# Talking-heads attention and a gated feed-forward in one kernel: one more of a group's blocks split for fp32r, and bulk transfers moved within a step

## The chip, the cores and the metric

One core of one Trainium2 chip. The metric is the device time of one execution in microseconds (us). The core has a TensorE (PE, with its weight loads as PEld), a VectorE (DVE), a ScalarE (ACT), a GpSimd (POOL) and a SyncE (SP). Nearly all transfers of this kernel are issued by SP, one after the other, on one queue.

## The reference

What must be computed, cut to what matters: attention in which the scores of the 12 heads are mixed before the softmax and the probabilities are mixed after it, and a feed-forward with a piecewise quadratic gate on the result.

```python
# q, k, v: (4, 12, 448, 64); w_pre, w_post: (12, 12); w_in: (768, 2048); w_out: (2048, 768)
scores = q @ k^T / 8
scores = einsum('bhij,hg->bgij', scores, w_pre)      # first mixing
attn = softmax(scores, axis=-1)                      # minus the max, exp, over (sum + 1e-9)
attn = einsum('bhij,hg->bgij', attn, w_post)         # second mixing
x = (attn @ v), heads side by side                   # (1792, 768)
h = x @ w_in
g = where(h >= 1, h, where(h <= -1, 0, (h + 1)**2 / 4))
out = g @ w_out
```

## The kernel before

**Tiles, blocks, groups, steps.** The queries are cut into 16 tiles (`tiles`): three of 120 and one of 88 for each of the four batches. A tile's scores for all heads (`scores`, L169) are computed with the queries on the partitions and copied to a buffer `ssb`, half of the copies by DVE (L187) and half by ACT (L189). For the first mixing the rows must lie otherwise: ten queries times twelve heads on 120 partitions. `load_s` (L198) does that by a transfer from `ssb` to a tile `s10` (named s in the profile), one for each block of ten queries, 210 KB. A tile has 12 blocks (9 for the short ones), and each third of a tile is a group of 4 (or 3) blocks. There are 48 groups, and the loop at L893 works on one group in each step n.

**The first mixing** (`pre`, L214) multiplies a block by a 120x120 matrix that holds w_pre. It comes in two forms. A block as loaded is multiplied in fp32 (L223; two TensorE instructions in the trace). A block that DVE has split into a high and a low part of type fp32r (`split`, L205: a cast at L210 and a subtraction at L211) takes three fp32r matmuls (L221). Before the change, the blocks 1 and 3 of each group of 4, and block 1 of each group of 3, are split; the first group has no split blocks.

**One step n**, in the order in which its parts are issued (each engine takes its own in this order):

1. SP: `load_s` for the blocks of group n+1, in the order 1, 3, 0, 2.
2. PE: `pre` of the blocks of group n, in the order 0, 1, 2, 3, and transposes of keys and queries (`at`).
3. SP: loads of raw keys and queries for later (`mid`), then `conv_load(n+1)`, 768 KB of int64 weights.
4. DVE: the row maxima of group n (L226), then the split of the first of group n+1's blocks.
5. PE: `visit`, the product with v (`pv`, L306 and L311), which needs the double PSUM bank that DVE's copy of the last scores (L187) has freed; then the last 64 keys of the second mixing (L276).
6. ACT: exp (L232) and the scaling of the weights; POOL and DVE: 1/sum (L239) and the second mixing's matrices scaled by it (L243).
7. ACT and DVE: `turned` and `copies` (transposed keys and queries, split too; L166 is DVE's half for the queries), then DVE: the other splits of group n+1.
8. PE and ACT: `post`, the second mixing of group n-1 (L260, L262); then `conv_rest(n)` on ACT, DVE and POOL (L373 to L377).
9. SP: `conv_store(n-1)` (L381), 384 KB that POOL's L377 finished.
10. PE, DVE, ACT: `scores` of a third of the next tile (`vis`), with DVE's copy L187.
11. SP: `late`: `load_q` and `load_v` for later tiles, and `store_x` of a finished tile.

`conv_load` and its kin turn the int64 weights into fp32 ones in a DRAM buffer; they run in most of the steps, but not where the keys of the next batch are loaded. The loop's last steps (from n = 44, where `early` is false) also load the feed-forward's operands. After it comes the feed-forward (L547 and L712), in fp32r matmuls throughout.

**The start.** Before the loop, keys and queries of tile 0 are loaded, its scores computed, and v of batch 0 loaded (three calls of `load_v(0, g)`, L130 and L133: 384 KB and two of 32 KB each). Then comes `load_s` for group 0. v of batch 0 is first read by `pv` in step 4. `load_v` writes the tile in which the first keys lay.

The buffers: `s10` has 8, the split halves `sh` and `sl` 2 each, the PSUM ring `ps_l` has 6 banks, and the double bank of `pair` is one.

```python
for m in (*groups[n + 1][1::2], *groups[n + 1][::2]):
    load_s(m)
...
for m in ms:
    pre(m)
nxt = list(groups[n + 1][1::2]) if n + 1 < NG else []
...
if nxt:
    split(nxt.pop(0))
...
for m in nxt:
    split(m)
```

Of the kernel before, what the change touches and what calls it, by code (L numbers as in the profile page):

```python
# [9 lines left out]
F32 = mybir.dt.float32  # L10
F32R = mybir.dt.float32r
# [11 lines left out]
def tile_talking_heads_moe(  # L23
# [12 lines left out]
    B, H, S, D = q.shape  # L36
# [5 lines left out]
    KM = IB * H  # L42
# [16 lines left out]
    ap_ = s_att.enter_context(tc.tile_pool(name="att", bufs=2))  # L59
# [15 lines left out]
    for b in range(B):  # L75
        for i0 in range(0, S, QT):
            n = min(QT, S - i0)
            tiles.append((b, i0, n, -(-n // IB)))
    blocks = []
    groups = []  # L80
# [6 lines left out]
    NG = len(groups)  # L87
# [30 lines left out]
    def load_q(t, gs=(0, 1)):  # L118
        b, i0, n, nb = tiles[t]
        if 0 in gs:  # L120
            qraw[t] = qp.tile([128, H, D], F32, tag="qraw", name="qraw", bufs=2)
        for g in gs:
            h = slice(g * HP, (g + 1) * HP)
            nc.sync.dma_start(out=qraw[t][:n, h], in_=q[b, h, i0:i0 + n].rearrange("h p d -> p h d"))

    def load_v(b, g):
        t = ap_.tile([128, 4 * KC * D + 2 * D], F32, tag=f"v{g}", name=f"v{g}", bufs=1)
        x = t[:, :4 * KC * D].rearrange("p (h c) -> p h c", h=4)
        y = t[:, 4 * KC * D:].rearrange("p (s d) -> p s d", d=D)
        nc.sync.dma_start(out=x, in_=v[b, 4 * g:4 * g + 4, :SM].rearrange("h (p r) d -> p h (r d)", r=KC))  # L130
        for m in range(2):
            h = 4 * g + 2 * m
            nc.sync.dma_start(out=y[half[m]], in_=v[b, h:h + 2, SM:].rearrange("s p d -> p s d"))  # L133
        vt[b, g] = x, y
# [56 lines left out]
    s10 = {}  # L191
# [6 lines left out]
    def load_s(m):  # L198
        t, o, ni, c = blocks[m]
        n, nb = tiles[t][2:]  # L200
        x = ap_.tile([KM, S], F32, tag="s10", name="s10", bufs=8)
        nc.sync.dma_start(out=x[:ni * H], in_=ssb[t][o:n:nb])
        s10[m] = x

    def split(m):  # L205
        k = blocks[m][2] * H
        x = s10.pop(m)
        hi = ap_.tile([KM, S], F32R, tag="sh", name="sh", bufs=2)
        lo = ap_.tile([KM, S], F32R, tag="sl", name="sl", bufs=2)
        nc.vector.tensor_copy(out=hi[:k], in_=x[:k])  # L210
        nc.vector.tensor_tensor(out=lo[:k], in0=x[:k], in1=hi[:k].bitcast(F32), op=ALU.subtract)  # L211
        s10[m] = (hi, lo)
# [52 lines left out]
    def post_rest(ms):  # L265

        t, o, ni, c0 = blocks[ms[0]]
        a = place(t)[1]
        ps = ps_l.tile([128, HG, 2, 4 * IB], F32, tag="l", name="ps_r")
        n = 0  # L270
        for m in ms:
            t, o, ni, c = blocks[m]
            w = wr[m].rearrange("p (g m s) i -> p m g s i", m=2, s=2)
            n = c - c0 + ni
            for x, p in enumerate(half):
                nc.tensor.matmul(out=ps[p, :, :, c - c0:n], lhsT=ex[m][:, SM:], rhs=w[:, x, :, :, :ni],  # L276
                                 start=True, stop=True)

        def out():
            nc.scalar.activation(out=a[:, :, c0:c0 + n], in_=ps.rearrange("p g s c -> p (g s) c")[:, :, :n],  # L280
                                 func=AF.Copy)
        return out
# [13 lines left out]
    def pv(t, g, step):  # L296
        b, i0, n, nb = tiles[t]
        if g == 0:
            xo[t] = ap_.tile([128, HP, QT], F32, tag="xo", name="xo", bufs=2)
        ps = banks_x(step)  # L300
        to = [ps[0][:, m, :] for m in range(2)] if len(ps) == 1 else ps
        a, ar = aT[t]
        x, xr = vt[b, g]
        for s in range(2):
            for m, p in enumerate(half):
                nc.tensor.matmul(out=to[m][half[s], :n], lhsT=xr[p, s, :], rhs=ar[p, 2 * g + s, :n],  # L306
                                 start=True, stop=False)
        for m in range(2):
            for r in range(KC):
                for s in ((0, 1), (1, 0))[r % 2]:  # L310
                    nc.tensor.matmul(out=to[m][half[s], :n], lhsT=x[:, 2 * m + s, r * D:(r + 1) * D],  # L311
                                     rhs=a[:, r, 4 * g + 2 * m + s, :n], start=False, stop=(r == KC - 1))

        full = n - (IB - 1) * nb

        def out():
            for i, p in enumerate(ps):
                to = xo[t][:, 2 * g:2 * g + 2, :nb * IB]
                if len(ps) == 2:
                    to = to[:, i:i + 1]  # L320
                    p = p.unsqueeze(1)
                to = to.rearrange("p m (a o) -> p m a o", o=nb)
                nc.scalar.activation(out=to[:, :, :, :full],
                                     in_=p[:, :, :full * IB].rearrange("p m (o a) -> p m a o", a=IB),
                                     func=AF.Copy)
                if full < nb:
                    x = to[:, :, :IB - 1, full:]
                    y = p[:, :, full * IB:n].rearrange("p m (o a) -> p m a o", a=IB - 1)
                    nc.scalar.activation(out=x, in_=y, func=AF.Copy)
        return out  # L330

    def visit(n, rests):
        v = [lambda x=x: pv(*x, n) for x in vis2.pop(n, ())]
        if rests:
            v.insert(len(v) if n < NE else 0, lambda: post_rest(rests))
        return [f() for f in v]
# [46 lines left out]
    def conv(n, f):  # L383
        if n in CS and CS.index(n) < 2 * NF:
            f(CS.index(n))
# [372 lines left out]
    with tc.manual_schedule():  # L758
# [38 lines left out]
        for g in range(3):  # L797
            scores(0, [2 * g, 2 * g + 1], g == 1)
            if g < 2:
                for hp in range(2 * g + 2, 2 * g + 4):  # L800
                    trans_k(0, hp)()()
        for g in range(3):
            load_v(0, g)
        for g in range(2):
            trans_q(1, g)()()
        for m in groups[0]:
# [18 lines left out]
        mid = {}  # L825
        late = {}

        def put(n, f):
            late.setdefault(n, []).append(f)

        vis = {}
        vis2 = {}
        for g in range(2):
            put(0, lambda g=g: load_q(2, (g,)))
        for t in range(1, len(tiles)):
# [57 lines left out]
        for n in range(NG + 2):  # L893
            if n == NE:
                s_qk.close()
                s_se.close()
                pool['w'] = ctx.enter_context(tc.tile_pool(name="ffw", bufs=2, side="right",
                                                           reuse_waits="tile"))
                pool['ps_h'] = ctx.enter_context(tc.tile_pool(
                    name="ps_h", bufs=1, space=PSUM, side="right", reuse_waits="tile"))  # L900
            if n == NG - 1:
                s_ss.close()
            ms = groups[n] if n < NG else ()
            old = list(groups[n - 1]) if 0 < n <= NG else []
            if n + 1 < NG:
                for m in (*groups[n + 1][1::2], *groups[n + 1][::2]):
                    load_s(m)
            for f in loads.get(n, ()):
                f()
            if ms:  # L910
                sm = ap_.tile([KM, 4], F32, tag="sm", name="sm", bufs=3)
                nm = ap_.tile([KM, 4], F32, tag="nm", name="nm", bufs=3)
            for m in ms:
                pre(m)
            nxt = list(groups[n + 1][1::2]) if n + 1 < NG else []
            turned = [f() for f in [f() for f in at.pop(n, ())]]
            for f in mid.pop(n, ()):
                f()
            conv(n + 1, conv_load)
            for m in ms:  # L920
                row_max(m, nm[:, m - ms[0]:m - ms[0] + 1])
            if n == NG - 1:
                w0_lo()
            if nxt:
                split(nxt.pop(0))
            rests = list(old)
            early = n < NE
            copies = visit(n, rests) if early else ()
            for j, m in enumerate(ms):
                if j == 3 and old and not early:  # L930
                    post(old.pop(0))
                exps(m, j, sm)
            conv(n, conv_scaled)
            if ms:
                norm(ms, sm)
            for f in (*turned, *copies):
                f()
            for m in nxt:
                split(m)
            if n == NG:  # L940
                step(0)
            for m in old:
                post(m)
            conv(n, conv_rest)
            conv(n - 1, conv_store)
            if not early:
                for f in visit(n, rests):
                    f()
            for t, hps in vis.pop(n, ()):
                scores(t, hps)  # L950
            for f in late.pop(n, ()):
                f()
# [10 lines left out]
        for j in range(NJ):  # L963
# [70 lines left out]
            f = j - NJ + 3  # L1034
# [73 lines left out]
```

## Time and profile before

| | us |
|---|---|
| median of 3 runs | 874.63 |
| the three runs | 870.09, 874.63, 876.0 |
| the profiled execution, its own time | 873.21 |
| its span, first to last instruction | 871.5 |
| PE busy | 854.1 (98% of the span) |
| DVE busy | 645.1 (74%) |
| ACT busy | 565.2 (65%) |
| POOL busy | 212.4 (24%) |
| mean granted TensorE clock | 0.998 of full speed |

The profiled execution lies 1.4 us under the median. Matmuls are pipelined and their ends are modelled, so the time that one matmul takes is read from the starts of those that follow each other, not from its length. The attention steps run from 23.6 us to about 450 us of the span, the feed-forward from there to the end.

### The profile page before, as it was taken

The page shows a single profiled execution, that of the slowest core. Times are in us where ns is not written, and L with a number is a line of the kernel's source. Part 1 is how long each engine was busy: PE and PEld are TensorE (multiplying, and loading weights), DVE is VectorE, ACT ScalarE, POOL GpSimd, SP SyncE. Part 2 cuts the span into 40 slices and gives each one's busy share as a digit, 9 for nine tenths or more (in the row PEclk, how much of TensorE's full clock was granted, in tenths as well). Part 3 has the DMA queues.
Part 4 walks back from the last instruction along what each step waited for, and adds up shares of the span by engine and source line. Part 5 has one row for each costly group of instructions (what it writes and reads, how often), then busy time and mean ns, then how long its engine had stood idle before and what let it go on. Part 6 is the DMA issues. An engine that isn't in the chain of part 4 may idle for free.

```text
span 871.5 us, 19952 instructions
## 1 busy us (share of the span) xinstructions
PE 854.1 (98%) x7848; PEld 734.2 (84%) x7848; DVE 645.1 (74%) x938; ACT 565.2 (65%) x1171; POOL 212.4 (24%) x269
## 2 busy tenths in 40 slices
PE   8999999999999999899999999999999999999998
PEld 6678777778787787687778788899999999999998
DVE  4887577775777767768578977997668978777853
ACT  3778788787887778778666466676667434433431
POOL 0366245653356533457320000000000000000000
PEclk9999999999999999999999999999999999999999
DMA  7888679986699876897556655654435544123331
GB/s 162 235 233 231 200 202 259 280 242 197 194 264 274 252 214 162 258 272 252 192 168 177 241 181 179 212 181 127 127 109 163 170 157 137 55 90 111 109 128 63
DMA packets 155329, 162.47 MB, mean 186 GB/s; under 512 B 66916, under 2 KB 148964, under 8 KB 155236
## 3 DMA queue, kind: packets, MB, share of 16 engines
q1 hardware_dynamic: 152404, 160.51, 61.1%
q8 instruction: 62, 1.02, 0.5%
q10 hardware_dynamic: 2832, 0.69, 0.4%
q14 instruction: 31, 0.25, 0.1%
HBM read 88.81 MB, written 33.82 MB: 141 GB/s over the span
## 4 chain that ended last, share of the span: by engine, by line
PE 86%; DMA 6%; DVE 3%; ACT 2%; SPq 2%; issue 1%; ACTq 0%; POOL 0%; DVEq 0%
PE ps_f L712 23%; PE ps_f L547 21%; PE ps_a L260 10%; PE ps_l L223 8%; PE ps_q L311 5%; DMA s<-ssb 5%; PE ps_l L221 5%; PE ps_q L180 3%; PE ps_s L180 3%; PE ps_r L276 2%; PE ps_q L306 1%; DMA k<-in_k_dram 1%; PE ps_t L161 1%; PE ps_k L141 1%; SPq L133 1%
## 5 line engine op out<-in xcount | busy, mean ns | idle before, releaser
L243 POOL TENSOR_SCALAR wr<-wpost,rs 120x120 f32<-120x120 f32 x180 | 141.4, 801 | 63.5 <-DVE rs L239 47.5
L232 ACT ACTIVATE e<-ps_l,nm 120x448 f32<-120x448 f32 x180 | 112.4, 632 | 60.9 <-DVE nm L226 59.6
L260 PE MATMUL ps_a<-wr,e 120*64 120x120 f32 (+1 forms) x2160 | 118.9, 266 | 0.0
L226 DVE TENSOR_REDUCE nm<-ps_l 120x1 f32<-120x448 f32 x180 | 105.7, 619 | 15.6 <-PE ps_l L223 11.4
L260 PEld LDWEIGHTS ps_a<-wr,e 120*64 120x64 f32 x2160 | 110.2, 137 | 2.6 <-issue 2.6
L695 ACT ACTIVATE sgh_p<-gq_p 128x1024 fp32r<-128x1024 f32 (+1 forms) x56 | 53.3, 953 | 89.7 <-PE ps_f L712 89.5
L223 PE MATMUL ps_l<-s,wpre 120*120 120x448 f32 x196 | 94.9, 569 | 5.8 <-DMA s<-ssb 3.8
L439 DVE SCALAR_TENSOR_TENSOR wl<-wi,wh 128x768 fp32r<-128x768 f32 x71 | 67.8, 954 | 41.9 <-ACT wh L436 41.9
L712 PE MATMUL ps_f<-wh,sgh_p 128*128 128x384 f32 x294 | 98.2, 334 | 0.0
L712 PE MATMUL ps_f<-wh,sgl_p 128*128 128x384 f32 x294 | 98.2, 334 | 0.0
L712 PE MATMUL ps_f<-wl,sgh_p 128*128 128x384 f32 x294 | 98.2, 334 | 0.0
L436 ACT ACTIVATE wh<-wi 128x768 fp32r<-128x768 f32 x71 | 59.7, 842 | 57.9 <-DVE wi L659 18.0
L262 ACT ACTIVATE aT<-ps_a 128x360 f32<-128x360 f32 x180 | 80.7, 494 | 13.7 <-PE ps_a L260 4.7
L696 DVE TENSOR_TENSOR sgl_p<-gq_p,sgh_p 128x1024 fp32r<-128x1024 f32 (+1 forms) x56 | 60.9, 1089 | 35.7 <-ACT sgh_p L695 35.7
L210 DVE CAST sh<-s 120x448 fp32r<-120x448 f32 (+1 forms) x82 | 33.2, 405 | 56.5 <-DMA s<-ssb 56.3
L187 DVE COPY ssb<-ps_q 120x896 f32<-120x896 f32 (+1 forms) x46 | 49.9, 1085 | 26.7 <-PE ps_q L180 26.7
L189 ACT ACTIVATE ssb<-ps_s 120x448 f32<-120x448 f32 (+1 forms) x96 | 47.2, 547 | 20.2 <-PE ps_s L180 17.8
L377 POOL TENSOR_TENSOR wt<-wt,wk 128x768 int32<-128x768 int32 x32 | 58.3, 1821 | 7.7 <-ACT wk L373 7.7
L221 PE MATMUL ps_l<-sh,wpre_h 120*120 120x448 f32 (+1 forms) x82 | 59.1, 721 | 0.0
L712 PEld LDWEIGHTS ps_f<-wh,sgl_p 128*128 128x128 f32 x294 | 55.2, 188 | 0.0
L712 PEld LDWEIGHTS ps_f<-wh,sgh_p 128*128 128x128 f32 x294 | 55.2, 188 | 0.0
L712 PEld LDWEIGHTS ps_f<-wl,sgh_p 128*128 128x128 f32 x294 | 55.2, 188 | 0.0
(235 smaller groups left out, 1943.3 us busy)
## 6 DMA issues: line engine op xcount, KB each, us to landing
s<-ssb SPq DMA_DIRECT2D x172, 210.0 KB
wraw<-in_moe_w_in_dram SPq DMA_DIRECT2D x16, 768.0 KB
wraw<-in_moe_w_out_dram SPq DMA_DIRECT2D x16, 768.0 KB
wi<-wod SPq DMA_DIRECT2D x29, 384.0 KB
wi<-wsd SPq DMA_DIRECT2D x28, 384.0 KB
wsd<-wt SPq DMA_DIRECT2D x16, 384.0 KB
wod<-wt SPq DMA_DIRECT2D x16, 384.0 KB
wi<-wss SPq DMA_DIRECT2D x16, 384.0 KB
```

The lines of the kernel that those rows point to most:

```text
L221: nc.tensor.matmul(out=lps[m], lhsT=w[:k], rhs=y[:k], start=(j == 0), stop=(j == 2))
L223: nc.tensor.matmul(out=lps[m], lhsT=wpre[:k], rhs=x[:k], start=True, stop=True)
L226: nc.vector.tensor_reduce(out=nm, in_=lps[m], axis=AX.X, op=ALU.max, negate=True)
L232: nc.scalar.activation(out=e, in_=ps, func=AF.Exp, bias=nm, accum_out=sm[:, j:j + 1])
L243: nc.gpsimd.tensor_scalar_mul(out=w[:, :, :ni], in0=wpost[:, :, :ni], scalar1=rs[:, j:j + 1])
L260: nc.tensor.matmul(out=ps[half[s], r, :ni * H], lhsT=e[:, c0:c0 + 64], rhs=w[:, :, :ni], start=True, stop=True)
L262: nc.scalar.activation(out=a[:, :, :, c:c + ni], in_=ps[:, :, :ni * H].rearrange("q r (h i) -> q r h i", h=H), func=AF.Copy)
L436: nc.scalar.activation(out=hi, in_=t, func=AF.Copy, scale=2.0 ** -8)
L439: nc.vector.scalar_tensor_tensor(out=lo, in0=t, scalar=2.0 ** -8, in1=hi.bitcast(F32), op0=ALU.mult, op1=ALU.subtract)
L547: nc.tensor.matmul(out=o, lhsT=u[:, c, k], rhs=x, start=first and r == 0 and m == 0, stop=r == 2 and m == 2, skip_group_check=True)
L696: nc.vector.tensor_tensor(out=lo, in0=src, in1=hi.bitcast(F32), op=ALU.subtract)
L712: nc.tensor.matmul(out=o, lhsT=x[:, f, c], rhs=y[:, f % 2, :], start=first and f == 0 and m == 0, stop=hf == 1 and f == 3 and m == 2, skip ...
```

## The change

Five edits. (1) In each group all blocks but the first are split, where it was every second one: 3 of 4 and 2 of 3. (2) Rows are loaded in the order 1, 2, 3, 0, so that the block that isn't split comes last. (3) `s10` has 6 buffers where it had 8, and `sh` and `sl` 3 each where they had 2. (4) `conv_store(n-1)` moves from place 9 of the step up to place 3, ahead of `mid` and `conv_load`; `late` moves in the early steps from place 11 up to the end of place 5. (5) The three `load_v(0, g)` move from the start into the places 3 of the steps 0, 1 and 2.

```diff
@@ load_s, split
-        x = ap_.tile([KM, S], F32, tag="s10", name="s10", bufs=8)
+        x = ap_.tile([KM, S], F32, tag="s10", name="s10", bufs=6)
...
-        hi = ap_.tile([KM, S], F32R, tag="sh", name="sh", bufs=2)
-        lo = ap_.tile([KM, S], F32R, tag="sl", name="sl", bufs=2)
+        hi = ap_.tile([KM, S], F32R, tag="sh", name="sh", bufs=3)
+        lo = ap_.tile([KM, S], F32R, tag="sl", name="sl", bufs=3)
@@ the start
-        for g in range(3):
-            load_v(0, g)
         for g in range(2):
             trans_q(1, g)()()
...
+        for g in range(3):
+            mid[g] = [lambda g=g: load_v(0, g)]
@@ the loop over the steps
             if n + 1 < NG:
-                for m in (*groups[n + 1][1::2], *groups[n + 1][::2]):
+                for m in (*groups[n + 1][1:], groups[n + 1][0]):
                     load_s(m)
...
             for m in ms:
                 pre(m)
-            nxt = list(groups[n + 1][1::2]) if n + 1 < NG else []
+            nxt = list(groups[n + 1][1:]) if n + 1 < NG else []
             turned = [f() for f in [f() for f in at.pop(n, ())]]
+            conv(n - 1, conv_store)
             for f in mid.pop(n, ()):
                 f()
             conv(n + 1, conv_load)
...
             copies = visit(n, rests) if early else ()
+            if early:
+                for f in late.pop(n, ()):
+                    f()
             for j, m in enumerate(ms):
...
             conv(n, conv_rest)
-            conv(n - 1, conv_store)
             if not early:
                 for f in visit(n, rests):
                     f()
```

## Rows read from the trace of the kernel before

**Rows 1.** The page: busy time of the engines.
```profile
PE 854.1 (98%) x7848; PEld 734.2 (84%) x7848; DVE 645.1 (74%) x938; ACT 565.2 (65%) x1171; POOL 212.4 (24%) x269
```
**Rows 2.** Windows: stretch, its length, engines' busy us, PEclk, DMA share, GB/s.
```profile
139.00:184.00 45.00, 42.84 (x539) 32.93 (x539) 32.40 (x61) 33.55 (x85) 26.79 (x29) 1.00 0.91 267
222.00:253.00 31.00, 31.00 (x422) 24.76 (x421) 25.64 (x46) 27.41 (x68) 17.52 (x20) 1.00 0.75 221
```
**Rows 3.** The page: the chain that ended last, by engine.
```profile
PE 86%; DMA 6%; DVE 3%; ACT 2%; SPq 2%; issue 1%; ACTq 0%; POOL 0%; DVEq 0%
```
**Rows 4.** PE's timeline inside one step: start, length, what, idle before.
```profile
201.62 0.91 PE L223 MATMUL ps_l<-s,wpre 120*120 120x448 f32 x2
...
202.58 0.37 PE L221 MATMUL ps_l<-sh,wpre_l 120*120 120x448 f32 x1
202.78 0.36 PE L221 MATMUL ps_l<-sl,wpre_h 120*120 120x448 f32 x1
202.99 0.82 PE L141 MATMUL ps_k<-ident,kraw 128*128 128x128 f32 x6
```
**Rows 5.** PE's timeline: the first group, all in fp32.
```profile
23.62 3.27 PE L223 MATMUL ps_l<-s,wpre 120*120 120x448 f32 x8
26.81 0.46 PE L180 MATMUL ps_q<-kh,qh 64*120 64x448 f32 x2
```
**Rows 6.** Groups: the split's two instructions on DVE; count, busy, mean, idle before.
```profile
L211 DVE TENSOR_TENSOR sl<-s,sh 120x448 fp32r<-120x448 f32 (+1 forms) x82 | 52.0, 634 | 2.8
...
L210 DVE CAST sh<-s 120x448 fp32r<-120x448 f32 (+1 forms) x82 | 33.2, 405 | 56.5 <-DMA s<-ssb 56.3
```
**Rows 7.** SP's timeline at the start.
```profile
13.26 0.42 SPq L130 DMA_DIRECT2D v<-in_v_dram  x1
13.73 1.34 SPq L133 DMA_DIRECT2D v<-in_v_dram  x2
...
28.18 3.42 SPq L202 DMA_DIRECT2D s<-ssb  x4
...
32.27 3.46 SPq L202 DMA_DIRECT2D s<-ssb  x4
```
**Rows 8.** DVE's timeline in step 2.
```profile
40.82 0.40 DVE L210 CAST sh<-s 120x448 fp32r<-120x448 f32 x1 [2.65 <-DMA s<-ssb]
```
**Rows 9.** PE's timeline at the end of step 2.
```profile
42.43 0.46 PE L180 MATMUL ps_q<-kh,ql 64*120 64x448 f32 x2 [1.15 <-DVE ql L166]
```
**Rows 10.** PE's timeline: waits ahead of a step's first mixing.
```profile
162.03 0.98 PE L223 MATMUL ps_l<-s,wpre 120*120 120x448 f32 x2 [1.20 <-ACT ssb L189]
...
272.21 0.98 PE L223 MATMUL ps_l<-s,wpre 120*120 120x448 f32 x2 [1.47 <-DMA s<-ssb]
...
356.05 1.82 PE L223 MATMUL ps_l<-s,wpre 120*120 120x448 f32 x2 [2.34 <-DMA s<-ssb]
...
358.79 1.20 PE L223 MATMUL ps_l<-s,wpre 120*120 120x448 f32 x2
```
**Rows 11.** DVE's timeline in the step before the last of these waits.
```profile
352.31 0.39 DVE L210 CAST sh<-s 120x448 fp32r<-120x448 f32 x1 [3.17 <-DMA s<-ssb]
...
353.71 0.51 DVE L210 CAST sh<-s 120x448 fp32r<-120x448 f32 x1 [0.27 <-DMA s<-ssb]
```
**Rows 12.** Windows: the us in which that wait ends.
```profile
356.00:357.00 1.00, 0.95 (x3) 0.56 (x3) 1.00 (x2) 0.00 (x0) 1.00 (x2) 0.50 0.68 233
```
**Rows 13.** DVE's timeline: the copy of scores in a late step.
```profile
153.67 1.08 DVE L187 COPY ssb<-ps_q 120x896 f32<-120x896 f32 x1
```
**Rows 14.** PE's timeline: the product with v that needs the bank.
```profile
155.05 0.38 PE L306 MATMUL ps_q<-aR,v 64*64 64x88 f32 x8
```
**Rows 15.** SP's timeline in step 3: a bulk load and a bulk store.
```profile
44.92 1.18 SPq L358 DMA_DIRECT2D wraw<-in_moe_w_in_dram  x1
47.69 2.36 SPq L381 DMA_DIRECT2D wsd<-wt  x1
```
**Rows 16.** Waits of SP: total us, times, longest.
```profile
SPq L381 <- POOL wt L377: 4.4, 3, 3.3
```

## The prediction

> **What bounds the kernel now.** I read the page's busy times first: PE is busy for 98% of the span, DVE for 74% [rows 1]. So the question for each edit is whether it takes work off PE or makes PE wait. The chain that ended last agrees, but not wholly: PE has 86% of it, and DMA 6% [rows 3]. Next come the windows by stretch, where the reader is to see that the attention isn't one regime. In some stretches PE has no gap at all (31.00 us busy of 31), with DVE at 25.64 of 31; in others, where v and the keys of the next batch are loaded, the transfers run at a share of 0.91 and PE has gaps (42.84 of 45) [rows 2]. PE's timeline at these gaps shows who makes it wait: three of the four gaps ahead of a step's first mixing are in the rows, of 1.20, 1.47 and 2.34 us, the fourth is shorter [rows 10]. Two of the four are put down to rows of scores that hadn't landed; the other two to ACT's copy of scores, and I take them for the same thing, since they end about one row's spacing after DVE's own wait for rows. The feed-forward, the second half, isn't touched.
>
> **The first mixing on PE.** The change splits one more block in each of the groups 1 to 47 (in groups of four 3 for 2, in groups of three 2 for 1), so 47 blocks change their form. From start to start, a block in fp32 and the first fp32r matmul of the next one take 202.58 - 201.62 = 0.96 us, and the fp32r matmuls behind it start 0.20 and 0.21 apart [rows 4]. So fp32 costs 0.96 - 0.205 = 0.755 and the split form 3 x 0.205 = 0.615: 0.14 us less, 6.6 us for 47. The first group, all in fp32, needs (26.81 - 23.62)/4 = 0.80 a block [rows 5]; by that it is 0.185 and 8.7 us. I take 0.14, because in the changed kernel as in this one the fp32 block has split ones behind it. It all arrives only where PE has no gap. I count some 15 steps in which a wait sets the next start (the first five, and ten around the three batch changes); there the saving turns into a longer wait. That leaves 32 x 0.14 = **4.5 us gained**, with 6.6 and 0 as ends.
>
> **The splits on DVE.** Each costs 405 + 634 = 1.04 us [rows 6], so 47 of them 49 us of DVE time. In the stretch from 222 to 253, with four steps, DVE would go from 25.64 to 29.8 of 31 us [rows 2], so it still fits, barely. In each step the added split is in the second batch of splits, behind 1/sum, and ahead of the weights' bit work and of the copy of scores (L187) that frees the double bank. PE wants that bank for the product with v. In an undisturbed step the copy is done some 2 us ahead. In steps in which DVE was itself held by a late row, it is close: the copy ends at 153.67 + 1.08 = 154.75, and PE starts the product at 155.05 [rows 13, 14], 0.30 us of cover for 1.04 us of delay. That makes 0.7 us of waiting. I see three steps of this kind (54.8, 155.1 and 183.9): **2.1 us lost**; the ends are 0 (if the later rows absorb it) and some 8 (if half a us is lost in each of 16 steps that wait for rows).
>
> **The order of the rows.** The block in fp32 is the first that PE takes in a step, and its row, third of four before, is now the last. Rows are issued 3.42/4 = 0.85 us apart [rows 7] and land 1.40 apart where the queue is full (352.31 and 353.71) [rows 11]. In the four steps in which PE waits for this row, the wait grows by one spacing: 4 x 0.85 to 4 x 1.40, 3.4 to 5.6 us, and 0 if the queue is less full than now. I take 0.85, as the edit to the store (below) holds bulk back behind these rows: **3.4 us lost**.
>
> **v of batch 0 in steps 0 to 2.** The place that it leaves was free: SP had no rows to load until the scores were there. The place that it gets isn't: one `load_v` occupies SP for 0.42 + 1.34, with the gap 1.81 us [rows 7], and SP has no pause there: the rows of group 2 are issued by 28.18 + 3.42 = 31.60, those of group 3 from 32.27 on, with one bulk load in between [rows 7]. Two of the three now stand ahead of the rows of group 3. Those rows already set the pace: DVE waits 2.65 us for the first, until 40.82 [rows 8], and the split of the queries behind it makes PE wait 1.15 us at 42.43 [rows 9]. So 2 x 1.81 = **3.6 us lost**; the ends are 0 (the shorter queue lands its rows sooner) and 7 (all three loads, and a lower clock after the wait). I keep the middle, as the wait is likely to be shared by two places: the last row of group 2, which PE needs at the start of step 2, moves too.
>
> **Edits that I cost at nothing.** `late` moved up: in the early steps no instruction of SP lies between its old and its new place but the store, which moves too, so SP's order is the same. The store ahead of the bulk load: the load must now wait for POOL as well, up to the 2.77 us between 44.92 and 47.69 [rows 15]; SP waits for that POOL result three times, 4.4 us in all [rows 16]. It is covered since the weights are needed a step (9 us) later; 3 us if that cover fails, and nothing below 0, since the bytes ahead of the next group's rows are the same. Six buffers for rows: they come free with the split of the group before, before SP comes to them; 0 to 1 us, and no gain, as fewer buffers start nothing earlier.
>
> **The sum.** -4.5 + 2.1 + 3.4 + 3.6 = +4.6 us. On the profiled execution that makes 873.2 + 4.6 = 877.8; the median lies 1.4 us above that execution, so 874.6 + 4.6 = **879**.
>
> **Rivals.**
> *The waits stay covered, and the PE work is a net gain.* For it: PE is 98% busy, and the saving is a matter of arithmetic; a queue that is full for 0.91 of a stretch [rows 2] still has places in which v may fit. Against it: the loads of v land in a stretch in which SP has no pause. It decides if the rows of group 3 land no later than 41.3, from where PE's present wait starts. Price: -6.6, or -8.7 by the first group's price: 866 to 868.
>
> *A longer wait lowers the clock.* After the 2.34 us without work, the granted clock was 0.50 (the 1.2 GHz level) [rows 12], and a pair of blocks took 358.79 - 356.05 = 2.74 us [rows 10], where at the full clock the same pair takes 202.99 - 201.62 = 1.37 [rows 4]: 1.4 us on top of the wait. After the 1.47 us at 272 the clock stayed. One spacing more at 162 and 272, and the wait in step 2, may bring three such falls: 3 x 1.4 = 4.2, and with the larger spacing (2.2 more) 879 + 6.4 = 885.
>
> *DVE becomes the bound.* If the lag that a late row gives DVE is no longer worked off, since a stretch's DVE work is now up to 29.8 us of 31, the waits for the bank recur: the 8 us of above for 2.1, 885.
>
> *The queue is full, and PE's saving is worth nothing.* If in all stretches with a share near 0.9 the rows come no sooner, whatever PE saves, the 4.5 us go too: 883.5. The Trainium skill has a rule for that on the page DMA: Bandwidth & Descriptors, section "Why a DMA increments its semaphore by 16 and not by 1": a transfer is spread over the largest number of engines up to 16 that divides the slowest dimension on both sides. By that rule a row transfer (10 queries there, 120 partitions here) would use ten engines, and a mean share of 0.91 would mean that these ten are full; no row here shows the engines one by one.
>
> **How the numbers follow.** My forecast (877 to 882) has 0.45, the first rival 0.20, the lower clock 0.17, DVE 0.08, the full queue 0.10. A change of 1% (865.9 or 883.4) is about what three runs of this kernel, 0.7% apart, can tell. Under 865.9 lies a third of the first rival, 0.07. Over 883.4 lie the clock's and DVE's cases (0.25) and half of the full queue's (0.05): 0.30. In between 0.63. The range runs from the first rival's 868 to the 885 of the clock's and DVE's cases with some of both, 890.
>
> **What would show it.** Right, if between 60 and 130 us, and in other stretches without gaps, steps are 0.14 us shorter; if L221 counts 129 blocks and L223 51; if PE's wait around 42 grows by some 3 us; if the waits of before at 162, 272 and 356 grow by about a us each; if DVE is busy for some 49 us more. Wrong, if PE's waits in the first 50 us stay as they are, or if the first mixing in the split form costs more than 0.62 us when one follows the other, which no row of before shows.

## The result, and the profile after

The changed kernel takes 881.47 us (median of 6 runs, 878.23 to 882.63), the one before 874.08 (6 runs, 870.09 to 876.47) in the same sittings. The ratio is 1.0089, with a 95% interval from 1.0063 to 1.0116: 7.8 us slower, and clear of noise. The forecast was 879, slightly slower, in a range from 868 to 890. Below, a ratio is turned into us by 874; each has an interval of some 0.25% to either side, so a difference of two ratios is good to about 3 us.

The profiled execution took 882.63 us (span 880.9). Its page, the busy times, the chain that ended last, and the two groups of the split (count, busy, mean, idle before):

```profile
PE 851.2 (97%) x7895; PEld 745.7 (85%) x7895; DVE 686.9 (78%) x1032; ACT 557.9 (63%) x1171; POOL 222.2 (25%) x269
...
PE 61%; DVE 12%; DMA 11%; ACT 9%; SPq 3%; issue 3%; POOL 1%; ACTq 0%; DVEq 0%
...
L211 DVE TENSOR_TENSOR sl<-s,sh 120x448 fp32r<-120x448 f32 x129 | 82.0, 636 | 4.4
...
L210 DVE CAST sh<-s 120x448 fp32r<-120x448 f32 x129 | 51.7, 401 | 39.5 <-DMA s<-ssb 39.3
```

The change did what it says: 129 splits for 82. Beside [rows 1], PE has 2.9 us less to do and DVE 41.8 us more. The row that tells most is the chain: PE had 86% of it before [rows 3] and has 61% now, and DVE's part went from 3 to 12%, the transfers' from 6 to 11. PE is no longer alone on the path.

PE's timeline in two stretches: split blocks of one group's first mixing, and the starts of two steps that follow each other without a gap.

```profile
59.32 0.37 PE L221 MATMUL ps_l<-sh,wpre_h 120*120 120x448 f32 x1
...
59.93 0.36 PE L221 MATMUL ps_l<-sh,wpre_h 120*120 120x448 f32 x1
...
60.54 0.39 PE L161 MATMUL ps_t<-ident,qraw 88*128 88x88 f32 x3
...
123.56 1.01 PE L223 MATMUL ps_l<-s,wpre 120*120 120x448 f32 x2
131.40 1.01 PE L223 MATMUL ps_l<-s,wpre 120*120 120x448 f32 x2
```

Split blocks that follow each other start 0.61 us apart, as worked out from [rows 4]. The step at 123.56 takes 7.84 us; the same step took 7.97 before (116.90 to 124.87). So PE's saving is there, 0.13 us a step. What it is up against is in PE's waits (engine and line, waited for whom, total us, times, longest):

```profile
PE ps_l L223 <- DMA s<-ssb: 11.9, 10, 2.6
PE ps_l L223 <- ACT ssb L189: 1.7, 2, 1.1
PE ps_t L161 <- ACT e L232: 1.6, 3, 0.8
...
PE ps_q L306 <- DVE ssb L187: 1.3, 4, 0.4
```

Before, the first two were these, and the last two didn't exist:

```profile
PE ps_l L223 <- DMA s<-ssb: 3.8, 2, 2.3
PE ps_l L223 <- ACT ssb L189: 1.9, 2, 1.2
```

Where the waits of the changed kernel stand is seen in PE's timeline (compare [rows 9, 10]):

```profile
37.11 0.98 PE L223 MATMUL ps_l<-s,wpre 120*120 120x448 f32 x2 [1.73 <-DMA s<-ssb]
...
44.64 0.47 PE L180 MATMUL ps_q<-kh,qh 64*120 64x448 f32 x2 [1.33 <-ACT qh L165]
46.19 0.47 PE L180 MATMUL ps_q<-kh,ql 64*120 64x448 f32 x2 [1.08 <-DVE ql L166]
...
47.89 1.82 PE L223 MATMUL ps_l<-s,wpre 120*120 120x448 f32 x2 [0.42 <-DMA s<-ssb]
...
279.86 1.82 PE L223 MATMUL ps_l<-s,wpre 120*120 120x448 f32 x2 [2.32 <-DMA s<-ssb]
...
365.50 1.82 PE L223 MATMUL ps_l<-s,wpre 120*120 120x448 f32 x2 [2.61 <-DMA s<-ssb]
```

Laid side by side, the start of step 4 has moved from 51.69 to 57.88, so 6.2 us are lost in the first four steps. From there to step 12 the distance is between 5.9 and 7.1 us and falls by 0.13 a step where nothing waits. Around the three batch changes it goes from 6.5 to 6.6 us (steps 12 to 20), from 6.2 to 9.8 (steps 23 to 32) and from 9.3 to 10.1 (steps 36 to 40); at the end of the span it is 9.4. At 47.89, 279.86 and 365.50 the first mixing takes 1.82 us where it takes 1.01: the granted clock has fallen, as in [rows 12], but at three places where it was one. The first of them by the us (the granted clock is the third number from the end):

```profile
48.00:49.00 1.00, 1.00 (x3) 0.58 (x3) 0.97 (x3) 0.49 (x2) 1.00 (x2) 0.50 0.90 313
```

### The profile page after: what moved, and what is told of

Read it like the earlier page. It is cut to its first block, busy times and chain, and to the rows that moved or that the text cites. A ratio compares the mean times of both kernels' runs of the same rounds, so it can differ in the third digit from the quotient of the medians.

```text
span 880.9 us, 20145 instructions
## 1 busy us (share of the span) xinstructions
PE 851.2 (97%) x7895; PEld 745.7 (85%) x7895; DVE 686.9 (78%) x1032; ACT 557.9 (63%) x1171; POOL 222.2 (25%) x269
## 4 chain that ended last, share of the span: by engine, by line
PE 61%; DVE 12%; DMA 11%; ACT 9%; SPq 3%; issue 3%; POOL 1%; ACTq 0%; DVEq 0%
PE ps_f L712 23%; PE ps_f L547 21%; DMA s<-ssb 8%; PE ps_a L260 5%; ACT e L232 4%; DVE ssb L187 2%; PE ps_l L223 2%; PE ps_l L221 2%; PE ps_q L311 2%; DVE wt L375 2%; DVE sl L211 2%; DVE sh L210 1%; PE ps_s L180 1%; PE ps_q L180 1%; DVE nm L226 1%
## 5 line engine op out<-in xcount | busy, mean ns | idle before, releaser
L243 POOL TENSOR_SCALAR wr<-wpost,rs 120x120 f32<-120x120 f32 x180 | 149.3, 846 | 43.2 <-DVE rs L239 28.1
L226 DVE TENSOR_REDUCE nm<-ps_l 120x1 f32<-120x448 f32 x180 | 103.3, 616 | 10.1 <-PE ps_l L223 8.6
L211 DVE TENSOR_TENSOR sl<-s,sh 120x448 fp32r<-120x448 f32 x129 | 82.0, 636 | 4.4
L262 ACT ACTIVATE aT<-ps_a 128x360 f32<-128x360 f32 x180 | 77.9, 504 | 10.8 <-PE ps_a L260 3.9
L210 DVE CAST sh<-s 120x448 fp32r<-120x448 f32 x129 | 51.7, 401 | 39.5 <-DMA s<-ssb 39.3
L223 PE MATMUL ps_l<-s,wpre 120*120 120x448 f32 x102 | 52.9, 607 | 14.3 <-DMA s<-ssb 11.9
L221 PE MATMUL ps_l<-sh,wpre_h 120*120 120x448 f32 x129 | 65.7, 509 | 0.0
L187 DVE COPY ssb<-ps_q 120x896 f32<-120x896 f32 (+1 forms) x46 | 49.9, 1084 | 12.7 <-PE ps_q L180 12.6
L238 POOL TENSOR_SCALAR rs<-sm 120x4 f32<-120x4 f32 (+1 forms) x48 | 13.7, 284 | 171.8 <-ACT e L232 171.8
```

The source lines that it names most:

```text
L187: nc.vector.tensor_copy(out=ssb[t][:n, h:h + 2, :], in_=wide[:n, :, :S])
L221: nc.tensor.matmul(out=lps[m], lhsT=w[:k], rhs=y[:k], start=(j == 0), stop=(j == 2))
L223: nc.tensor.matmul(out=lps[m], lhsT=wpre[:k], rhs=x[:k], start=True, stop=True)
L226: nc.vector.tensor_reduce(out=nm, in_=lps[m], axis=AX.X, op=ALU.max, negate=True)
L243: nc.gpsimd.tensor_scalar_mul(out=w[:, :, :ni], in0=wpost[:, :, :ni], scalar1=rs[:, j:j + 1])
L262: nc.scalar.activation(out=a[:, :, :, c:c + ni], in_=ps[:, :, :ni * H].rearrange("q r (h i) -> q r h i", h=H), func=AF.Copy)
```

## The experiments

Twelve kernels were run, each timed in five rounds beside the kernel before. The lines of the diffs are against the changed kernel unless it is said otherwise.

| kernel | ratio to before | 95% interval | median us |
|---|---|---|---|
| changed | 1.0089 | 1.0063 to 1.0116 | 881.47 |
| v_at_start | 1.0040 | 1.0017 to 1.0063 | 878.09 |
| row0_not_last | 1.0145 | 1.0121 to 1.0170 | 886.46 |
| splits_alone | 1.0164 | 1.0143 to 1.0186 | 888.00 |
| store_back | 1.0096 | 1.0072 to 1.0120 | 882.78 |
| two_splits | 1.0002 | 0.9980 to 1.0025 | 873.97 |
| idle_split | 1.0083 | 1.0051 to 1.0115 | 880.31 |
| third_on_pool | 1.0074 | 1.0048 to 1.0100 | 880.19 |
| third_on_act_pool | 0.9987 | 0.9965 to 1.0009 | 871.97 |
| v_alone | 1.0070 | 1.0045 to 1.0095 | 879.63 |
| seven_rows | 1.0021 | 1.0000 to 1.0041 | 877.12 |
| act_pool_seven | 0.9977 | 0.9954 to 1.0000 | 872.68 |
| act_pool_seven_store | 1.0023 | 1.0002 to 1.0043 | 876.44 |

### v_at_start: the loads of v back where they were

```diff
+        for g in range(3):
+            load_v(0, g)
         for g in range(2):
             trans_q(1, g)()()
...
-        for g in range(3):
-            mid[g] = [lambda g=g: load_v(0, g)]
```

> The changed kernel with the three loads of v back at the start, before the rows of group 0. Theory (rows come late: v in steps 0 to 2 and row 0 last): step 4 begins some 4 us sooner than in the changed kernel (57.88 there, 51.69 before), and the whole is 4 us shorter, about 1.004 of before. Rival (DVE's extra splits set the time): the start is DVE's, step 4 still begins after 56, and the time stays within 1 us of the changed kernel's, 1.009.

1.0040: 4.3 us shorter than the changed kernel. Step 4 begins 0.8 us behind that of before, where it was 6.2. This is the theory's number; the rival, in which the start is DVE's, falls. In the changed kernel SP's timeline shows the way (beside [rows 7]):

```profile
27.07 0.49 SPq L130 DMA_DIRECT2D v<-in_v_dram  x1
27.63 1.35 SPq L133 DMA_DIRECT2D v<-in_v_dram  x2
...
30.28 3.50 SPq L202 DMA_DIRECT2D s<-ssb  x4
33.82 0.49 SPq L130 DMA_DIRECT2D v<-in_v_dram  x1
34.37 1.35 SPq L133 DMA_DIRECT2D v<-in_v_dram  x2
...
36.52 3.74 SPq L202 DMA_DIRECT2D s<-ssb  x4
```

Group 3's rows are issued at 36.52 instead of 32.27, 4.25 us later: two loads of v at 1.9 us each, and some 0.4 us more. DVE casts the first of them at 44.58 instead of 40.82 [rows 8], after a wait of 3.99 us. So the place on SP set the delay.

### v_alone: only the loads of v moved, in the kernel before

```diff
-        for g in range(3):
-            load_v(0, g)
...
+        for g in range(3):
+            mid[g] = [lambda g=g: load_v(0, g)]
```

> The kernel before with only the three loads of v moved into steps 0, 1 and 2. Theory (the loads stand ahead of rows that set the pace): 3 to 4.5 us longer, 1.004 to 1.005, all of it before step 5. Rival (v costs only because DVE is late with the added splits): within 1 us of before, 0.999 to 1.001.

1.0070: 6.1 us longer, so more than the expected 3 to 4.5, and the rival falls: v costs without the added splits too. Step 5 begins 5.2 us late in the profile, and the distance stays at 5.2 for nine more steps. (The profiled execution, 876.50, is the shortest of twelve, so its whole span says less.) PE's timeline has the waits, the first at the last row of group 2, the others behind the rows of groups 3 and 4:

```profile
36.23 0.98 PE L223 MATMUL ps_l<-s,wpre 120*120 120x448 f32 x2 [1.79 <-DMA s<-ssb]
...
37.72 1.70 PE L223 MATMUL ps_l<-s,wpre 120*120 120x448 f32 x2
...
54.44 0.55 PE L180 MATMUL ps_s<-kh,qh 64*120 64x448 f32 x1 [1.23 <-DVE ql L166]
55.90 1.82 PE L223 MATMUL ps_l<-s,wpre 120*120 120x448 f32 x2 [0.16 <-DMA s<-ssb]
```

The lengths of 1.70 and 1.82 us, at 37.72 and 55.90, show what the expectation left out: the granted clock is 0.50 from 38 to 41 and from 55 to 58. At the 1.4 us that the prediction gives for one such fall, 2.8 of the 5.2 us are the clock's, by estimate. None of the twelve executions had a mean granted clock above 0.998.

### store_back: the bulk store back at the end of the step

```diff
-            conv(n - 1, conv_store)
             for f in mid.pop(n, ()):
...
             conv(n, conv_rest)
+            conv(n - 1, conv_store)
```

> The changed kernel with the bulk store back at the end of the step, behind the bulk load in SP's order. Theory: no more than 1 us either way, 1.008 to 1.010 of before. Rival (the store ahead of the load holds back the load, and so the rows behind both): 3 us shorter, 1.005.

1.0096, 0.6 us above the changed kernel: no difference that can be told, as the theory has it.

### row0_not_last: the row of the unsplit block last but one

```diff
-                for m in (*groups[n + 1][1:], groups[n + 1][0]):
+                for m in (*groups[n + 1][1:-1], groups[n + 1][0], groups[n + 1][-1]):
```

> The changed kernel with row 0 issued last but one (1, 2, 0, 3 in groups of four; 1, 0, 2 in groups of three). Theory (row order): PE's waits ahead of the first mixing for rows (11.9 us in ten waits) fall by about 0.85 us each, 3 to 6 us, about 1.004 of before. Rival (DVE): the last split now waits for the last row, DVE's wait for rows grows from 39 us, and the time stays or gets longer, 1.009 to 1.013.

1.0145: 4.9 us longer, not 3 to 6 us shorter. The theory falls here and the rival stands. PE's waits, and DVE's timeline in one step:

```profile
PE ps_q L306 <- DVE ssb L187: 13.3, 16, 1.5
PE ps_t L161 <- ACT e L232: 3.6, 3, 1.6
...
PE ps_l L223 <- DMA s<-ssb: 1.9, 3, 0.9
```

```profile
83.86 0.46 DVE L210 CAST sh<-s 120x448 fp32r<-120x448 f32 x1 [0.80 <-DMA s<-ssb]
84.35 0.66 DVE L211 TENSOR_TENSOR sl<-s,sh 120x448 fp32r<-120x448 f32 x1
84.94 0.55 DVE L374 TENSOR_SCALAR wt<-wt 128x768 int32<-128x768 int32 x1
85.52 0.96 DVE L375 SCALAR_TENSOR_TENSOR wt<-wraw,wt 128x768 int32<-128x768 int32 x1
86.40 1.08 DVE L187 COPY ssb<-ps_q 88x896 f32<-88x896 f32 x1
```

PE's wait for its own row did shrink, from 11.9 to 1.9 us. But now the last split waits for the last row (0.80 here), everything behind it on DVE is late, and PE waits 13.3 us in 16 steps for the copy (L187) that frees the bank. In the changed kernel that wait is 1.3.

### splits_alone: only the splits and buffers, in the kernel before

```diff
-        x = ap_.tile([KM, S], F32, tag="s10", name="s10", bufs=8)
+        x = ap_.tile([KM, S], F32, tag="s10", name="s10", bufs=6)
...
-                for m in (*groups[n + 1][1::2], *groups[n + 1][::2]):
+                for m in (*groups[n + 1][1:-1], groups[n + 1][0], groups[n + 1][-1]):
...
-            nxt = list(groups[n + 1][1::2]) if n + 1 < NG else []
+            nxt = list(groups[n + 1][1:]) if n + 1 < NG else []
```

(and 3 buffers for each half, as in the change).

> The kernel before with only the added splits and their buffers (rows 6, halves 3), rows in the order 1, 2, 0, 3; v, store and late loads where they were. Theory: PE's saving of some 4.5 us less 2 us for DVE's lag at the bank, 0.997 of before (872). Rival (DVE's extra splits set the time): 3 to 8 us slower, 1.004 to 1.009.

1.0164: 14 us longer than before, the slowest of all, beyond what either theory gave. Its waits are those of row0_not_last, with 16.3 us in 18 steps at the bank. It says that the splits are no gain by themselves in this order of rows; but it mixes the splits with the order, so the next pair takes the splits by themselves.

### two_splits and idle_split: the price on DVE and the gain on PE, each alone

Both have v at the start and rows in the order 1, 2, 3, 0. In idle_split DVE makes the added split and nobody reads it; block 2 is mixed in fp32 as loaded.

```diff
 two_splits:
-            nxt = list(groups[n + 1][1:]) if n + 1 < NG else []
+            nxt = list(groups[n + 1][1::2]) if n + 1 < NG else []
 idle_split:
-    def split(m):
+    def split(m, used=-1):
...
-        s10[m] = (hi, lo)
+        s10[m] = x if m == used else (hi, lo)
...
-                split(m)
+                split(m, groups[n + 1][2])
```

> The changed kernel with v at the start and only the splits of before (blocks 1 and 3, or 1); rows still in the order 1, 2, 3, 0, store and late loads still moved. It leaves out both DVE's added work and PE's saving. Theory (each added split costs more in waits than it saves on PE): 1.000 to 1.002 of before, so some 2 us shorter than with three splits (1.004). Rival (the row order costs, the splits are a net gain): 1.007 or more, longer than with three splits by the 4 to 6 us that PE no longer saves.

> As two_splits, but DVE makes the added split of block 2 as well and PE doesn't use it: block 2 is mixed in fp32 from the row as loaded. So DVE's work is that of the changed kernel and PE's that of before. Theory: 6 to 7 us longer than with the split used (1.004), 1.011 to 1.012, if PE's saving is worth all of its 6.6 us; the distance to two_splits is then what DVE's added work costs, some 8 us. Rival (PE's saving is swallowed by waits): the same time as with the split used, 1.004.

With v_at_start these make a ladder: 1.0002 with two splits, 1.0083 with the third made and not used, 1.0040 with the third made and used. DVE's added work costs 0.0081, 7.1 us, and PE's use of it gives back 0.0043, 3.8 us. (In idle_split the row of block 2 also stays in its buffer until PE has mixed it, so the 3.8 us hold what its earlier release is worth.) The clock isn't what makes the difference: two executions of idle_split at a mean granted clock of 1.000 took 878.47 and 880.19, five of two_splits 870.16 to 875.18.

two_splits, with the new row order, the moved store, the moved `late` and the other buffers, is as fast as before. That is the price of these edits together. It doesn't show that row 0 in the last place costs nothing: PE's waits for rows did grow in it, to 8.2 us from 3.8, and the store ahead of the bulk load may have given this back (it is worth 4.0 us in a kernel below). No kernel has the order by itself.

What the added work does to PE is in PE's waits, first in two_splits, then in idle_split:

```profile
PE ps_l L223 <- DMA s<-ssb: 8.2, 7, 2.4
```

```profile
PE ps_l L223 <- DMA s<-ssb: 10.5, 9, 2.3
...
PE ps_q L306 <- DVE ssb L187: 1.5, 4, 0.5
```

All of PE's waits between 24 and 455 us, summed from its timelines, are 10.8 us in two_splits, 16.9 in idle_split and 21.1 in v_at_start: the added work costs PE 6.1 us of waiting in these traces, near the 7.1 of the ratios. Of the 6.1, 2.3 are waits for rows and 1.5 for the bank, in the lines above; the rest is short waits in several places, for DVE's copy and ACT's exp among them.

DVE's lateness can reach the rows through SP. Rows are loaded from the buffer that DVE's copy fills, into a buffer that DVE's split has freed; the waits of SP ahead of a row, in the kernel before, in the changed one, and in two_splits:

```profile
SPq L202 <- DVE ssb L187: 59.5, 15, 10.9
...
SPq L202 <- DVE sh L210: 1.2, 2, 0.8
```

```profile
SPq L202 <- DVE ssb L187: 72.1, 22, 9.9
...
SPq L202 <- DVE nm L226: 11.9, 20, 1.0
...
SPq L202 <- DVE sh L210: 6.5, 10, 1.4
```

```profile
SPq L202 <- DVE ssb L187: 61.9, 19, 9.8
...
SPq L202 <- DVE nm L226: 13.0, 22, 1.1
...
SPq L202 <- DVE sh L210: 1.5, 2, 0.8
```

Over all of its waits ahead of rows, SP waits for DVE for 64 us in the kernel before, 90 in two_splits, 105 in idle_split and 99 in the changed kernel. So most of what was added comes with the other edits and costs no time (two_splits), and some 14 us come with the added splits. That these 14 are what makes PE's rows late is argued and not shown; no kernel tried it by itself.

### third_on_pool and third_on_act_pool: the last split of a group on other engines

```diff
-        nc.vector.tensor_copy(out=hi[:k], in_=x[:k])
-        nc.vector.tensor_tensor(out=lo[:k], in0=x[:k], in1=hi[:k].bitcast(F32), op=ALU.subtract)
+        if away:
+            nc.gpsimd.tensor_copy(out=hi[:k], in_=x[:k])
+            nc.gpsimd.tensor_tensor(out=lo[:k], in0=x[:k], in1=hi[:k].bitcast(F32), op=ALU.subtract)
+        else:
+            ...
-                split(m)
+                split(m, m == groups[n + 1][-1])
```

In third_on_act_pool the cast is `nc.scalar.activation(out=hi[:k], in_=x[:k], func=AF.Copy)`. Both have v at the start.

> The changed kernel with v at the start, and the last split of each group made by POOL, both instructions, so that DVE has the work of before again and PE keeps its saving. Theory (DVE's added work is what costs): 3 to 7 us shorter than with DVE's split (1.004), 0.996 to 1.000 of before. Rival (the rows' order and landing cost, not DVE): 1.004 stays; or POOL, with some 2 us more in each step, is late with the second mixing's matrices and it gets longer.

> As third_on_pool, but the cast by ACT and only the subtraction by POOL. Theory: as third_on_pool, 0.996 to 1.000, with POOL's part halved; ACT has some 0.5 us more in each step, behind the second mixing's first copies. Rival: ACT's place in its queue makes PE's banks free later, 1.004 or more.

The two differ by 8 us. With the cast on ACT it is 0.9987, 4.6 us shorter than with DVE's split: DVE's work was what cost. Against two_splits (1.0002), where the third split isn't made at all, it is 1.3 us, which can't be told from nothing. With both instructions on POOL it is 1.0074, longer than with DVE's. In third_on_pool's trace, the group of POOL's subtraction, PE's wait for it and SP's wait for it:

```profile
L212 POOL TENSOR_TENSOR sl<-s,sh 120x448 fp32r<-120x448 f32 (+1 forms) x47 | 53.9, 1147 | 4.0
```

```profile
PE ps_l L225 <- POOL sl L212: 6.5, 12, 0.6
```

```profile
SPq L202 <- POOL sl L212: 20.5, 16, 4.9
```

In the program's order POOL gets to the split only behind the second mixing's matrices, so the split is done late, frees its row late and holds up PE. Its profiled execution (874.75) is near the shortest of its runs (874.03 to 884.18, median 880.19), so this trace shows the kind of wait and not the whole of it.

### seven_rows, act_pool_seven, act_pool_seven_store: buffers, and the store again

```diff
-        x = ap_.tile([KM, S], F32, tag="s10", name="s10", bufs=6)
+        x = ap_.tile([KM, S], F32, tag="s10", name="s10", bufs=7)
```

seven_rows is v_at_start with that line, act_pool_seven is third_on_act_pool with it; act_pool_seven_store is the latter with the diff of store_back.

> The changed kernel with v at the start and 7 buffers for rows instead of 6 (8 don't fit). Theory A (six buffers tie the issue of rows to DVE's late splits, so that PE waits 12.7 us for row 0): PE's waits for rows fall to some 8 us and the time by 3 us or more, 1.000 to 1.001 of before. Theory B (DVE's own chain sets the rows' source, the copy of the scores, so buffers don't matter): the time stays at 1.004.

> third_on_act_pool with 7 buffers for rows. Theory A: 2 us shorter than with six (0.9987), 0.996. Theory B: the same as with six, 0.9987.

> act_pool_seven with the bulk store back behind the bulk load, as in the kernel before. Both theories: within 1 us of act_pool_seven, as the store's move was worth nothing in the changed kernel; a version that beats before clearly would be at 0.996 or less.

The seventh buffer gives 1.0021 for 1.0040, and 0.9977 for 0.9987. PE's waits for rows fall from 12.7 to 8.0 us, as theory A has it, but 1.7 and 0.9 us of time are inside the intervals: not settled.

act_pool_seven has the lowest ratio, 2.0 us shorter than the kernel before, with an interval that ends at 1.0000: it beats the changed kernel clearly, but it can't be told from the kernel before, nor from third_on_act_pool.

The store's place, which I had at nothing, is worth 4.0 us here: 1.0023 with it behind the bulk load, 0.9977 ahead of it. Both theories were wrong on that. The lines of both traces, SP's wait at the store and PE's wait for rows, first with the store ahead:

```profile
SPq L385 <- POOL wt L381: 40.3, 20, 5.8
...
PE ps_l L227 <- DMA s<-ssb: 3.2, 3, 1.6
```

```profile
SPq L385 <- POOL wt L381: 8.3, 5, 2.7
...
PE ps_l L227 <- DMA s<-ssb: 7.7, 7, 1.8
```

With the store ahead, SP waits for POOL there and issues the 768 KB behind it later, while the rows issued just before land; PE waits 4.5 us less for them. That the later bulk is the cause is my reading of these two lines, and no kernel tried it by itself.

## Why the prediction came out

It said 4.6 us slower and it is 7.8, inside the range. Its terms, as the runs have them:

**PE's saving: right.** 0.14 us a block was read from starts, the steps without a gap show 0.13; L221 counts 129 blocks and L223 51, as forecast. I took 4.5 of the 6.6 us as arriving; idle_split against v_at_start has 3.8 (good to some 3 us).

**v in the first steps: right in place and mechanism, a little small.** 3.6 us were forecast; undoing it in the changed kernel gives 4.3, doing it alone costs 6.1, with ends of 0 and 7. The wait did split over two places (37.11 and 44.64 to 47.89), as I had said, but the clock fell all the same at 48 us, which I had expected the split to avoid; by the prediction's price 1.4 us of the delay are that fall's, and v_alone has two of them.

**The splits on DVE: right in sign, mis-sized, 2.1 us for 7.1.** The step that failed is that the bank, which L187 frees, is the only place where DVE's lateness reaches PE. There PE waits 1.3 us in the changed kernel, 1.5 in idle_split and 2.7 in v_at_start, from none, which is about the 2.1 that I had. The runs show the rest elsewhere: in idle_split PE waits 6.1 us more than in two_splits, 2.3 of them for rows, and in the changed kernel its transposes wait for an exp that follows DVE's maxima (1.6 us, from none). That the rows are late because SP waits for DVE ahead of them fits SP's waits, but isn't shown by itself. My upper end of 8 us held it. I counted DVE as fitting into its stretch (29.8 of 31 us) and took that for cover. DVE's busy time grew by 41.8 us where I had 49; its two split groups alone grew by 48.5.

**The order of the rows: open.** I had 3.4 us lost, by one spacing for each wait of PE. PE's waits for rows did grow in two_splits, from 3.8 to 8.2 us, near the forecast; but two_splits takes the time of before, and whether the order costs nothing or the moved store pays for it can't be told. The sign that I gave for it failed: the waits at 162, 272 and 356 were to grow by about a us each, and they went from 1.20, 1.47 and 2.34 us to 0.81, 2.32 and 2.61. With three splits on DVE the last place is better than the last but one by 4.9 us (row0_not_last). There I had not asked who waits for the row that takes row 0's place: DVE's last split, with the whole of DVE's queue behind it.

**The sum.** The order and the edits at nothing were forecast at +3.4 us together and measure 0.2 (two_splits); DVE's splits were forecast at +2.1 and measure 7.1. The two misses, some 3 us too much and 5 too little, go opposite ways, so the sum came out nearer than its parts. That is luck.

**The edits at nothing.** The store's move is nothing in the changed kernel (0.6 us), though SP's waits for POOL ahead of it grew from 4.4 us to 26.7; I had said "nothing below 0", and in the kernel with DVE relieved and seven row buffers it is a gain of 4.0. `late` was not tried by itself. Six buffers instead of seven cost 1.7 us or nothing, which is open; the eight of before were not tried with the added splits.

**The rivals.** The lower clock took place, with two falls more than before in the profiled execution, 1.4 us each by the prediction's price; three other executions of the changed kernel had a mean granted clock of 0.998 to 1.000 and took 878.2 to 882.0, so it is a part of the 3 us over the forecast at most. That DVE becomes the bound was the rival nearest to what happened, though not by the waits for the bank that it named; I gave it 0.08. The full queue isn't borne out: idle_split against v_at_start shows a saving of 3.8 us with the same transfers. But that is only just clear of the intervals, and the 1.3 us of third_on_act_pool against two_splits are not. Nor does a mean share of 0.91 over 16 engines say that ten of them are full: it puts any ten at 0.86 or more.

## What to carry to other kernels

DVE, with a quarter of its time idle, wasn't free: ask for its queue what each instruction behind the added one releases (a bank, a buffer, the source of a transfer), not only whether the sum still fits. To price work that helps one engine and costs another, run the work with its result unused: the ladder of without, unused and used gives both prices. When the order of loads changes, ask who waits for the one that is now last: here a split on DVE, with its queue behind it, was the worse choice by 4.9 us. And when several edits move together and the time stays, don't put any one of them at nothing.

## What the hardware showed that I had not expected

The granted clock fell to 0.50 at 48 us, after waits of 1.33, 1.08 and 0.42 us with short pieces of work between them, none as long as the 2.34 us of [rows 10]; after a single wait of 1.73 (37.11) it did not. In idle_split a wait of the same 1.73 us was followed by 0.50, and so was one of 1.79 us in v_alone (36.23). So the length of the last wait alone doesn't tell here:

```profile
251.18 1.82 PE L223 MATMUL ps_l<-s,wpre 120*120 120x448 f32 x2 [1.73 <-DMA s<-ssb]
```

The same subtraction of 120x448 takes 0.636 us on DVE and 1.15 to 1.18 us on POOL, and the cast 0.40 on DVE, 0.58 on ACT and 0.59 on POOL (blocks of 108 partitions left out).
